# Sixteen short rows ahead: splitting the first load of a decode step's keys

## The chip, the core and the metric

The kernel runs on one core of one Trainium2 chip. The metric is the device time of one execution in microseconds, as the median of several runs. A profile of one execution stands beside it: what each engine did and when, and what moved through the DMA queues. The engines are PE (matrix products; PEld is its loading of weights), DVE, ACT, POOL, and SP, which here only issues transfers between HBM and the on-chip memory. That memory has 128 rows; a transfer writes a stretch of bytes into each of the rows that it names.

## The reference

One token for each of 4 sequences passes an attention block over a cache and an MLP, both with a residual. Everything is in float32.

```python
B, Sq, D = 4, 1, 448;  Hq, Hkv, Sk, Dh = 16, 8, 4096, 256
W = min(4096, max(256, Sk // 4))                       # 1024: the last keys and values only
q = (x @ wq).reshape(B, Sq, Hq, Dh).transpose(0, 2, 1, 3)
k = jnp.repeat(k_cache[:, :, Sk - W:, :], rep, axis=1)  # rep = 2 query heads for each of 8
v = jnp.repeat(v_cache[:, :, Sk - W:, :], rep, axis=1)
scores = jnp.einsum("bhqd,bhkd->bhqk", q, k) * (Dh ** -0.5)
o = jnp.einsum("bhqk,bhkd->bhqd", _softmax(scores), v)
...
h = x + A(_layernorm(x))            # A ends with: heads side by side, times wo
h2 = h + B(_layernorm(h))           # B: layernorm, gelu(y @ w1 + b1) @ w2 + b2
```

Keys and values of 8 heads and 1024 positions and the weights make 88.2 MB that are read once.

## The kernel before, in words

All data is packed on the host so that each load is a block of 128 rows. The 8 key and value heads are handled in four pairs. For a pair, PE forms the queries from `wq` (`project`, `queries`), multiplies them with the keys (`scores`), and DVE and ACT take the softmax (`softmax`, `transpose_p`). Then PE multiplies with the values (`values`) and with `wo` (`outputs`). After the last pair the MLP follows with `w1` and `w2`.

The loads go through three large slots of on-chip memory (`ring`, tiles `slot`). Each holds up to 65,024 bytes per row, and the loads take the slots in turn: `t0`, then `l1` to `l8`, then the last three (`te0` to `te2`) with the last keys and values, `wo`, `w1` and `w2`. All are issued by SP in program order. A load that reuses a slot waits on SP until PE has read what lay there. The first slot, `t0`, receives two loads: `wq0` (the query weights of head 0, and with them `x` and the two bias vectors, 7312 bytes per row), and behind it `k0` (the keys of head 0, 32768 bytes per row, and 6144 bytes with the first three quarters of the query weights of head 1). The rest of those weights comes in two small transfers of 32 rows x 2048 bytes into `wq1_last`. `l1` and `l2` follow into the other two slots and wait for nothing.

The order on each engine is the order of the code. A recorder (`Machine`) notes every operation with the parts of memory that it reads and writes, and `emit` gives each the semaphore waits that it needs. It follows a write by rows (in groups of four) and columns, and every transfer has a semaphore of its own (`landed_N`, N being the operation's number). So an operation that reads columns that two transfers wrote waits for both. All operations are emitted at line 75, which is why nearly all rows of the profile say L75; tiles tell them apart.

In the front of the program, `x` is normalised (`centred`, `column_mean`, `rsqrt`), the queries of heads 0 and 1 are formed, and the scores of head 0 begin:

```python
    t = slot("t0")
    wqt, xT, b2T, b1T = cut(load(t, 0, wq0), (WEIGHTS, ND * B, 4, 4 * 4))
    ...
    ka, kb, wqt1 = cut(load(t, WEIGHTS + COLUMNS, k0), (HALF, HALF, 3 * 512))
    ...
    project(pq, wq_parts(yT[1], wqt1, wq1_last), False)
    queries(0, pq)
    s = score_tiles(0)
    for h, kt in enumerate((ka, kb)):
        scores(s, 0, h, keys(kt))
```

Of the kernel before, what the change touches and what calls it, by code (L numbers as in the profile page):

```python
# [24 lines left out]
HALF = CACHE // 2  # L25
WEIGHTS = 4 * D
SLOT = CACHE + 2 * WEIGHTS + HALF
COLUMNS = ND * B + 4 + 4 * 4
# [169 lines left out]
        return flat.rearrange(f"p ({names}) -> p {names}", **{f"a{i}": n for i, n in enumerate(shape[1:])})  # L198


def block_kernel(nc, wq0, k0, wq1, l1, l2, l3, l4, l5, l6, l7, l8, k7, vo, v7, wo, w1, w2, out):
    real, nc = nc, Machine(nc)

    def rows_of_tag(name, shape, dtype):
# [16 lines left out]
    def slot(name):  # L221
        return ring.tile([P, SLOT], F32, tag="slot", name=name)

    def load(t, at, src, pieces=None):
        dst = t[:, at : at + src.shape[-1]]
        at = 0
        for n in pieces or (src.shape[-1],):
            nc.sync.dma_start(dst[:, at : at + n], src[:, at : at + n])
            at += n
        return dst  # L230

    def cut(t, sizes):
        parts, at = [], 0
        for n in sizes:
            parts.append(t[:, at : at + n])
            at += n
        return parts


    def wq_parts(y, t, last=None):  # L240
        parts = [(a, y[:, a, :], slice(0, 512), t[:, a * 512 : (a + 1) * 512]) for a in range(3)]
        if last is not None:
            return parts + [(3, y[:H, 3, :], slice(0, 512), last)]
        for i in range(2):
            parts.append((3, y[:, 3 + i, :], slice(i * 2 * P, (i + 1) * 2 * P), t[:, 3 * 512 :]))
        return parts
# [9 lines left out]
    def output_weights(t):  # L256
# [6 lines left out]
        out=ident, in_=ident, compare_op=ALU.not_equal, fill=1.0, base=0, pattern=[[-1, P]], channel_multiplier=1  # L263
# [187 lines left out]


    t = slot("t0")
    wqt, xT, b2T, b1T = cut(load(t, 0, wq0), (WEIGHTS, ND * B, 4, 4 * 4))
    wqt = wq_parts(yT[0], wqt)
    xT = xT.rearrange("p (a b) -> p a b", a=ND)
    ka, kb, wqt1 = cut(load(t, WEIGHTS + COLUMNS, k0), (HALF, HALF, 3 * 512))
    for i in range(2):
        nc.sync.dma_start(
            wq1_last[i * Q : (i + 1) * Q, :], wq1[i].rearrange("e (p c) -> e p c", c=512)[:, :4, :]  # L460
# [44 lines left out]
    ka, kb, va = cut(load(slot("l1"), 0, l1), (HALF, HALF, HALF))  # L505
# [8 lines left out]
    vb, v, wo_a, wo_b = cut(load(slot("l2"), 0, l2), (HALF, CACHE, WEIGHTS, WEIGHTS))  # L514
# [5 lines left out]
    wq_a, wq_b, ka, kb, k2 = cut(load(slot("l3"), 0, l3), (WEIGHTS, WEIGHTS, HALF, HALF, HALF))  # L520
# [7 lines left out]
    k2, v, wq_a, wq_b = cut(load(slot("l4"), 0, l4), (HALF, CACHE, WEIGHTS, WEIGHTS))  # L528
# [8 lines left out]
    v, wo_a, wo_b, ka = cut(load(slot("l5"), 0, l5), (CACHE, WEIGHTS, WEIGHTS, HALF))  # L537
# [6 lines left out]
    kb, ka, k2 = cut(load(slot("l6"), 0, l6), (HALF, HALF, HALF))  # L544
# [7 lines left out]
    v, va, wq_a, wq_b = cut(load(slot("l7"), 0, l7), (CACHE, HALF, WEIGHTS, WEIGHTS))  # L552
# [6 lines left out]
    vb, wo_a, wo_b, ka, kb = cut(load(slot("l8"), 0, l8), (HALF, WEIGHTS, WEIGHTS, HALF, HALF))  # L559
# [9 lines left out]
    v, wot = cut(load(e[1], 0, vo), (CACHE, 2 * D))  # L569
# [138 lines left out]
    for c in range(first, NFC - 1):  # L708
        g = gT[:, c, :] if c < 12 else gT_last[:, c - 12, :]
        for j in range(4):  # L710
            m, n = (Q, 2) if c == first else (B, 2 if j < 3 else 1)
# [5 lines left out]
    for part, of in ((0, slice(0, 3)), (1, slice(3, 4))):  # L717
        for j in range(4):
            n = P // 4 if j < 3 else H // 4
# [89 lines left out]
```

## Time and profile before

| what | value |
|---|---|
| time, median of 3 runs | 211.96 us (211.85 to 212.13) |
| time of the profiled execution | 211.87 us |
| its span, first to last instruction | 210.6 us |
| PE busy | 139.0 us (66%), 984 matmuls |
| DVE, ACT, POOL busy | 28.8, 14.4, 5.0 us |
| moved by DMA | 88.42 MB in 3400 packets, mean 420 GB/s |
| load of `wq0`, of `k0` | 914 KB in 4.8 us, 4864 KB in 15.9 us from issue to landing |

Times in views of the trace count from the start of the span. The two rows of digits for the DMA show the span in 40 equal slices: the busy share of the 16 DMA engines in tenths, and the GB/s that they moved. A packet is counted, with all its bytes, in the window or slice in which it starts, so short windows can show a share above 1. In rows of the timeline, what stands in brackets is how long the engine sat idle before, and what ended that.

### The profile page before, as it was taken

The numbers are of one execution on the slowest core, as the hardware profiler recorded it, in microseconds if no ns is written. First come the engines' busy times: TensorE is split into PE (matmuls) and PEld (weight loads), VectorE is DVE, ScalarE is ACT, GpSimd is POOL, SyncE is SP. The second block draws the span as 40 slices with busy tenths as digits, with TensorE's granted clock in tenths as the row PEclk, the third lists the DMA queues.
The fourth block names the chain that finished last, engine by engine and source line by source line (L and its number), as shares of the span: only waits on it lengthen the run. The fifth ranks groups of instructions, "written<-read, shape, count | busy, mean of one in ns | idle before, by whom it ended". The sixth has DMA issues, their size and how long they took to land.

```text
span 210.6 us, 2206 instructions
## 1 busy us (share of the span) xinstructions
PE 139.0 (66%) x984; PEld 47.2 (22%) x984; DVE 28.8 (14%) x135; ACT 14.4 (7%) x34; POOL 5.0 (2%) x17
## 2 busy tenths in 40 slices
PE   0467759621971679198359775419806999888996
PEld 0420202200220223034012222102301233224332
DVE  7210101300020011013001104000100213012320
ACT  2010000200000010020000002000100002010311
POOL 5100000000000000000000000000000000000100
PEclk9999996996799559969967999757965899999999
DMA  7999999899999999999999999999999999999993
GB/s 296 429 399 473 448 492 389 386 436 507 398 398 410 531 389 410 410 519 398 413 411 448 481 398 425 434 470 398 434 411 442 416 428 429 425 407 439 424 409 138
DMA packets 3400, 88.42 MB, mean 420 GB/s; under 512 B 512, under 2 KB 768, under 8 KB 1344
## 3 DMA queue, kind: packets, MB, share of 16 engines
q1 hardware_dynamic: 3392, 88.30, 97.6%
q8 instruction: 7, 0.11, 0.2%
q14 instruction: 1, 0.01, 0.0%
HBM read 88.23 MB, written 0.07 MB: 419 GB/s over the span
## 4 chain that ended last, share of the span: by engine, by line
DMA 77%; PE 18%; SPq 2%; DVE 1%; issue 1%; ACT 0%
DMA slot<-l 64%; DMA slot<-w 14%; PE b_o L75 9%; PE b_s L75 4%; PE b_acc L75 3%; SPq L75 2%; PE b_m L75 1%; DVE oT L75 1%; DVE w_o L75 0%; PE b_t L75 0%; DVE o_u L75 0%; ACT o_u L75 0%; DVE o_res L75 0%
## 5 line engine op out<-in xcount | busy, mean ns | idle before, releaser
L75 PE MATMUL b_o<-slot,pT 128*32 128x512 f32 x224 | 33.6, 752 | 29.3 <-DMA slot<-l 28.5
L75 PE MATMUL b_s<-slot,qT 128*32 128x512 f32 x256 | 36.6, 722 | 10.4 <-DMA slot<-l 9.1
L75 PE MATMUL b_m<-slot,yT 128*32 128x512 f32 (+1 forms) x76 | 11.9, 734 | 11.5 <-DMA slot<-l 6.4
L75 PEld LDWEIGHTS b_o<-slot,pT 128*32 128x32 f32 x224 | 7.8, 132 | 51.4 <-DMA slot<-l 30.9
L75 PE MATMUL b_t<-idle 128*32 128x512 bf16 x64 | 18.1, 404 | 0.5 <-DVE pT L75 0.5
L75 PEld LDWEIGHTS b_s<-slot,qT 128*32 128x32 f32 x256 | 8.8, 128 | 35.9 <-issue 22.5
L75 ACT ACTIVATE o_p<-b_s,w_nm 128x512 f32<-128x512 f32 x8 | 5.4, 682 | 93.1 <-DVE w_nm L75 93.1
L75 DVE TENSOR_REDUCE w_mx<-b_s 128x1 f32<-128x512 f32 x8 | 5.5, 692 | 43.7 <-PE b_s L75 43.7
L75 DVE TENSOR_SCALAR w_o<-b_o,w_rec 128x512 f32<-128x512 f32 x4 | 3.0, 751 | 52.5 <-PE b_o L75 52.5
L75 PEld LDWEIGHTS b_m<-slot,yT 128*32 128x32 f32 x76 | 4.3, 142 | 17.9 <-DMA slot<-l 6.9
L75 PEld LDWEIGHTS b_t<-idle 128*32 128x32 bf16 x64 | 5.9, 100 | 10.3 <-issue 5.8
L75 DVE TENSOR_REDUCE w_sm<-b_m 128x32 f32<-128x128 f32 x4 | 1.2, 291 | 48.2 <-PE b_m L75 48.2
L75 PE MATMUL b_t<-ident,o_p 128*128 128x128 f32 x32 | 5.0, 285 | 4.0 <-ACT o_p L75 3.9
L75 PE MATMUL b_acc<-slot,oT 128*32 128x448 f32 x52 | 6.1, 545 | 1.9 <-DVE oT L75 1.9
L75 ACT COPY w_qs<-b_m 128x512 f32<-128x512 f32 x4 | 2.3, 584 | 60.8 <-PE b_m L75 60.8
L75 POOL TENSOR_TENSOR o_r<-w_ve,mhalf 128x1 f32<-128x1 f32 x2 | 1.1, 542 | 189.0 <-DVE w_ve L75 189.0
L75 PE MATMUL b_m<-ident,w_qs 128*128 128x128 f32 x16 | 3.5, 361 | 2.9 <-ACT w_qs L75 2.9
L75 PEld LDWEIGHTS b_t<-ident,o_p 128*128 128x128 f32 x32 | 3.4, 141 | 7.4 <-ACT o_p L75 7.4
L75 PE MATMUL b_m<-slot,mean 128*128 128x12 f32 (+1 forms) x4 | 1.1, 370 | 5.6 <-DMA slot<-wq 5.6
L75 PE MATMUL b_o<-slot,yT 128*32 128x512 f32 x10 | 4.6, 594 | 0.0
L75 PE MATMUL b_m<-ident,w_o 128*128 128x128 f32 x20 | 3.3, 286 | 1.8 <-DVE w_o L75 1.8
L75 DVE COPY pT<-b_t 128x16 f32<-128x16 f32 x32 | 3.3, 167 | 6.0 <-PE b_t L75 6.0
(94 smaller groups left out, 66.7 us busy)
## 6 DMA issues: line engine op xcount, KB each, us to landing
slot<-l SPq DMA_DIRECT2D x6, 7936.0 KB, 43.0
slot<-l SPq DMA_DIRECT2D x2, 6144.0 KB, 34.1
slot<-k SPq DMA_DIRECT2D x1, 4864.0 KB, 15.9
slot<-vo SPq DMA_DIRECT2D x1, 4544.0 KB, 33.1
slot<-k SPq DMA_DIRECT2D x1, 4096.0 KB, 43.5
slot<-v SPq DMA_DIRECT2D x1, 3072.0 KB, 19.0
slot<-w SPq DMA_DIRECT2D x1, 2240.0 KB, 28.6
slot<-w SPq DMA_DIRECT2D x1, 1792.0 KB, 34.0
```

Of the source, the lines that this page charges most:

```text
L75: self.machine.add(Op(self.name, lambda: getattr(issuer, what)(*args, **kwargs), outs, ins, what))
```

## The change

The load `k0` is cut into three. Of the first 14336 bytes of each row (`kf`, the first 7 of 16 parts of the keys), 16 rows are loaded before `wq0`, and the other 112 rows behind it. The rest of the columns, 24576 bytes per row, follows as the new `k0`. They land in the same places as before, so what the engines read is unchanged.

```diff
     t = slot("t0")
+    n = kf.shape[-1]
+    k0t = t[:, WEIGHTS + COLUMNS :][:, : n + k0.shape[-1]]
+    nc.sync.dma_start(k0t[:16, :n], kf[:16])
     wqt, xT, b2T, b1T = cut(load(t, 0, wq0), (WEIGHTS, ND * B, 4, 4 * 4))
     wqt = wq_parts(yT[0], wqt)
     xT = xT.rearrange("p (a b) -> p a b", a=ND)
-    ka, kb, wqt1 = cut(load(t, WEIGHTS + COLUMNS, k0), (HALF, HALF, 3 * 512))
+    nc.sync.dma_start(k0t[16:, :n], kf[16:])
+    nc.sync.dma_start(k0t[:, n:], k0)
+    ka, kb, wqt1 = cut(k0t, (HALF, HALF, 3 * 512))
...
-        "wq0": np.concatenate([wq[0], xT, b2, b1], axis=1), "k0": k0, "wq1": wq1, ...
+        "wq0": np.concatenate([wq[0], xT, b2, b1], axis=1), "kf": k0[:, : 7 * 512], "k0": k0[:, 7 * 512 :], "wq1": wq1, ...
```

On SP, at the start of the program, the transfers stand so (rows x elements of 4 bytes; a minus is before, a plus is after):

```order
-L75 DMA slot<-wq 128x1828 [waits barrier_Pool_Activation_PE_DVE_SP_release]
-L75 DMA slot<-k 128x9728
+L75 DMA slot<-kf 16x3584 [waits barrier_Pool_Activation_PE_DVE_SP_release]
+L75 DMA slot<-wq 128x1828
+L75 DMA slot<-kf 112x3584
+L75 DMA slot<-k 128x6144
 L75 DMA wq_last<-wq 32x1x512 x2
 L75 DMA slot<-l 128x12288
```

The 16 rows take the place behind the start barrier, `wq0` is second, and all that follows is two issues later.

On PE, from the second head's query weights to the first scores (`b_m` holds the queries, `b_s` the scores; 26 is the landing of the 16 rows, 28 that of the 112, and `k0` has the number 27 before and 29 after):

```order
-L75 MATMUL b_m<-slot,yT 32x512 [waits landed_27]
+L75 MATMUL b_m<-slot,yT 32x512 [waits landed_29]
 L75 MATMUL b_m<-slot,yT 32x512 x2
-L75 MATMUL b_m<-wq_last,yT 32x512 [waits landed_28,landed_29]
+L75 MATMUL b_m<-wq_last,yT 32x512 [waits landed_30,landed_31]
 L75 MATMUL b_m<-ident,w_qs 128x128 [waits done_ACT]
 L75 MATMUL b_m<-ident,w_qs 128x128 x3
-L75 MATMUL b_s<-slot,qT 32x512 [waits done_DVE]
+L75 MATMUL b_s<-slot,qT 32x512 [waits landed_28,landed_26,done_DVE]
 L75 MATMUL b_s<-slot,qT 32x512 x15
```

The projection waits for the last of the pieces as it did for the whole, and the first score matmul has two waits more, for the two pieces of `kf`. No other instruction on PE, DVE, ACT or POOL has moved.

More of the change, by code (lines that the diff above doesn't have):

```diff
@@ L198, in tile, with block_kernel @@
         return flat.rearrange(f"p ({names}) -> p {names}", **{f"a{i}": n for i, n in enumerate(shape[1:])})
-def block_kernel(nc, wq0, k0, wq1, l1, l2, l3, l4, l5, l6, l7, l8, k7, vo, v7, wo, w1, w2, out):
+def block_kernel(nc, wq0, kf, k0, wq1, l1, l2, l3, l4, l5, l6, l7, l8, k7, vo, v7, wo, w1, w2, out):
     real, nc = nc, Machine(nc)
@@ L795 @@
     arrays = {
-        "wq0": np.concatenate([wq[0], xT, b2, b1], axis=1), "k0": k0, "wq1": wq1, **loads, "k7": k[7], "vo": vo, "v7": v[7], "wo": wo_end, "w1": w1, "w2": w2,
+        "wq0": np.concatenate([wq[0], xT, b2, b1], axis=1), "kf": k0[:, : 7 * 512], "k0": k0[:, 7 * 512 :], "wq1": wq1, **loads, "k7": k[7], "vo": vo, "v7": v[7], "wo": wo_end, "w1": w1, "w2": w2,
     }
```

## The prediction

> **What bounds the kernel now.** I read the page first: the slices, the DMA queues, the chain that ended last.
>
> ```profile
> DMA  7999999899999999999999999999999999999993
> GB/s 296 429 399 473 448 492 389 386 436 507 398 398 410 531 389 410 410 519 398 413 411 448 481 398 425 434 470 398 434 411 442 416 428 429 425 407 439 424 409 138
> q1 hardware_dynamic: 3392, 88.30, 97.6%
> DMA 77%; PE 18%; SPq 2%; DVE 1%; issue 1%; ACT 0%
> DMA slot<-l 64%; DMA slot<-w 14%; PE b_o L75 9%; PE b_s L75 4%; PE b_acc L75 3%; SPq L75 2%; PE b_m L75 1%; DVE oT L75 1%; DVE w_o L75 0%; PE b_t L75 0%; DVE o_u L75 0%; ACT o_u L75 0%; DVE o_res L75 0%
> ```
>
> The DMA engines are busy in 38 of 40 slices; one queue carries 88.3 MB and fills 97.6% of the span of 16 engines. The chain runs 77% of the span through loads. So the kernel is one stream of bytes, and PE works beside it. The stretches of the stream, from the view of busy time by window (last two columns: DMA share, GB/s):
>
> ```profile
> core 0: us, PE busy (x) PEld busy (x) DVE busy (x) ACT busy (x) POOL busy (x), PEclk, DMA share, GB/s
> 1.50:1.70 0.20, 0.00 (x0) 0.00 (x0) 0.17 (x2) 0.20 (x1) 0.20 (x2) 1.00 0.00 0
> 1.70:2.10 0.40, 0.00 (x0) 0.00 (x0) 0.37 (x3) 0.31 (x1) 0.40 (x4) 1.00 1.24 219
> 2.10:2.50 0.40, 0.00 (x0) 0.00 (x0) 0.40 (x3) 0.00 (x0) 0.40 (x2) 1.00 0.59 128
> 2.50:2.90 0.40, 0.00 (x0) 0.00 (x0) 0.40 (x1) 0.00 (x0) 0.40 (x2) 1.00 0.71 256
> 2.90:3.30 0.40, 0.00 (x0) 0.00 (x0) 0.40 (x1) 0.00 (x0) 0.40 (x2) 1.00 1.09 457
> 17.00:200.00 183.00, 125.03 (x847) 40.03 (x847) 21.52 (x103) 10.64 (x26) 0.89 (x2) 0.86 1.00 430
> 206.80:208.00 1.20, 1.20 (x48) 0.84 (x40) 0.00 (x0) 0.53 (x1) 0.00 (x0) 1.00 0.39 138
> ```
>
> From 17 to 200 us the stream has a share of 1.00 at 430 GB/s, which is 26.9 GB/s for each of 16 engines. It begins at 1.7 us, and it still moves bytes after 206.8. What waits for its end:
>
> ```profile
> 206.64 0.56 PEld L75 LDWEIGHTS b_o<-slot,gT 128*32 128x32 f32 x24 [0.63 <-DMA slot<-w]
> 207.85 0.73 PE L75 MATMUL b_o<-slot,gT_last 128*4 128x64 f32 x24
> 208.66 0.29 DVE L75 TENSOR_TENSOR o_res<-b_o,o_hb 128x128 f32<-128x128 f32 x1 [4.31 <-PE b_o L75]
> 208.97 0.35 SPq L75 DMA_DIRECT2D out<-o_res  x1
> ```
>
> The last matmuls use the last pieces of `w2`, some 0.7 us behind the last bytes, then come one addition and the store. Nothing lies between that could take up a delay: a stream that ends a microsecond later ends the kernel about a microsecond later. The profiled execution took 211.87 us with a span of 210.6, 0.09 under the median of 211.96; the sum is made against 211.87.
>
> **The change, part by part.** No byte is added. The order in the queue is changed, and one load of 4864 KB becomes three, of 16 rows x 14336 bytes, 112 rows x 14336 and 128 rows x 24576. Issues and waits in the front of the program:
>
> ```profile
> 0.73 0.39 SPq L75 DMA_DIRECT2D slot<-wq  x1
> 1.18 0.41 SPq L75 DMA_DIRECT2D slot<-k  x1
> 1.64 1.55 SPq L75 DMA_DIRECT2D wq_last<-wq  x2
> 3.23 39.24 SPq L75 DMA_DIRECT2D slot<-l  x4
> 17.13 1.93 PE L75 MATMUL b_m<-slot,yT 128*32 128x512 f32 x6 [3.33 <-DMA slot<-k]
> PE b_m L75 <- DMA slot<-wq: 5.6, 1, 5.6
> PE b_m L75 <- DMA slot<-k: 3.3, 1, 3.3
> PE b_s L75 <- DMA slot<-l: 2.3, 1, 2.3
> ```
>
> *Two more issues on SP.* An issue to all 128 rows takes 0.39 to 0.41 us, with 0.05 to the next, so `wq0` is issued 0.45 us later (1.18) and the pair for `wq1_last` and `l1` some 0.9 later (`l1` at 4.1). `l1` is needed in the queue when `wq0` and the keys are through: 5.92 MB at 430 GB/s are 13.8 us behind 1.7, so about 15.5. Eleven microseconds of queued work hide the later issues; `l2` follows directly, and all further loads wait for PE and not for SP's turn. Zero.
>
> *`wq0` lands later.* It holds `x` and the first weights, and PE waits 5.6 us for it. Behind the 16 rows it lands 0.5 to 2.2 us later. The normalisation and the first projection come after it, but then PE waits 3.3 us for the keys' load, whose tail holds the second weights: that wait is the cover, and up to 3.3 us cost nothing. Even beyond it, PE waits 2.3 us for `l1` after the first scores, and the slot of the first keys, which the third load needs, is next written when `l1` and `l2` are through (14.4 MB, 34 us at 430 GB/s). Zero.
>
> *A wait added on PE.* The first score matmul now waits for the landings of the 16 and of the 112 rows as well. Behind it stand all scores of PE. Both are ahead of the last piece in the queue, and the projections before the scores already wait for that piece. Zero, unless the last piece lands before them; the cover is then the 2.3 us above.
>
> *More packets.* Each engine moves 8 rows of a load to 128 rows. It gets 8 packets more (two short rows for a long one) and two landings more. The shortest packets of the stream, the 2 KB rows of `wq1_last`, show what a packet costs:
>
> ```profile
> DMA packets 19, 0.03 MB, mean 205 GB/s; under 512 B 3, under 2 KB 3, under 8 KB 19
> q1 hardware_dynamic: 19, 0.03, 53.6%
> ```
>
> These are the queue's rows for 16.20 to 16.36 us, where only 16 such packets and 3 landings start: 53.6% of 16 engines for 0.16 us is 1.37 us of packet time, 86 ns for each 2 KB at most, where 2048 bytes at 26.9 GB/s need 76. Some 10 ns for a packet, times 10: **+0.10 us**.
>
> *The start of the stream.* Between 1.7 and 3.3 us it moved 219, 128, 256 and 457 GB/s in steps of 0.4 us. Against 430 it lacks (211 + 302 + 174 - 27) x 0.4 = 264 KB, which is 0.61 us. This is all that an earlier or better filled start could win. With 16 rows, each engine can have one packet of 14336 bytes (0.53 us at 26.9 GB/s), about as long as the 0.45 us until the next issue. The gain has bounds of 0 and 0.61. I take all of it, **-0.61 us**, since whatever is slow in these 1.6 us now runs under a transfer that in my forecast takes longer than that anyway.
>
> *The 16 rows themselves.* No transfer of the trace goes to 16 rows. One end: all 16 engines carry a row each at 26.9 GB/s, 0.53 us. Other end: a row receives no more than in a transfer to 128 rows, 430/128 = 3.4 GB/s, which makes 54 GB/s for 16 rows and 229 KB in 4.27 us, 3.73 more. The nearest row is the one above: the transfer to 32 adjacent rows filled 8.6 of 16 engines and moved 205 GB/s, so 32 rows took the bytes of about eight engines, one for four rows, and nothing in the trace shows several engines writing into the same few rows at full rate. Sixteen rows at half of 205 are 102 GB/s: 2.24 us, **+1.70 us** over the 0.53. It is on the path, since every engine stands on its one row until then and the stream behind it moves back. [...]
>
> *The 112 rows.* At 430 GB/s 1.61 MB take 3.73 us; at the 128-row pace per row (376 GB/s) 4.27. Bounds 0 and, if they crowd as the 16 do, several microseconds. Nearest is the load to 128 rows, so I take the second value, **+0.53 us**.
>
> *The 128 rows of 24576 bytes* go at the stream's rate: zero beyond the packets counted.
>
> Sum: +0.10 - 0.61 + 1.70 + 0.53 = +1.72; 211.87 + 1.72 = **213.6 us**.
>
> **The rivals.** *The start is won (faster, the other side).* If 16 engines write their 16 rows side by side at 26.9 GB/s, nothing crowds, and each engine has work from 1.7 us on while `wq0` is issued: up to -0.61 + 0.10 = -0.51, 211.4 us. For it speak the weak 128 to 256 GB/s in the start, which look like engines without work, and that the row is as long as an issue. Against it, that the trace has no such transfer and the 0.61 must be won nearly whole. It decides when the 16 rows land in under about 0.7 us of stream.
>
> *The start is paid once (no change).* The slow 1.6 us may belong to the first bytes of any transfer into an empty queue. Then the 16 rows take the place of `wq0` in it, without crowding: +0.10 and at most 0.5 won, 211.6 to 212.0, 211.9 in the middle of what I hold likely. For it, the queue's rows of the first 1.2 us:
>
> ```profile
> DMA packets 33, 0.24 MB, mean 201 GB/s; under 512 B 0, under 2 KB 0, under 8 KB 33
> q1 hardware_dynamic: 33, 0.24, 84.7%
> ```
>
> In 1.7 to 2.9 us 33 packets account for 84.7% of the engines' time at half the rate: work is there and is slow. Against it: this does not tell waiting for a request from waiting for bytes.
>
> *The 112 rows crowd too.* Seven adjacent rows for an engine don't line up with groups of four; at half pace their 3.73 us double: 213.6 - 0.5 + 3.7 = 216.8 us.
>
> **How the numbers follow.** A change under 0.2% (0.42 us) can't be told from none here. The forecast, crowding by 16 rows, has 0.50: nothing shows the contrary, and it needs one mechanism. The won start 0.25, the start paid once 0.18, the heavier crowding 0.07. So slower 0.57, the same 0.18, faster 0.25. The forecast's own range: crowding half as strong, without the 112 rows (+0.85 - 0.4 + 0.1 = 0.5), 212.4, up to 2.24 us without any win at the start and with a share of 1.5 us on the 112 rows (+1.7 + 0.1 + 1.5), 215.2. For 8 in 10 the range goes down to the won start, 211.3, and stops at 215.2, which leaves out the heavy crowding and little else.
>
> **What would show it.** Right: in the first slice fewer GB/s, about 100 in the 2 us after the first bytes; the wait for `wq0` 7 us or more instead of 5.6; the keys landing at 18 to 19 us instead of 17.1; the chain of waits as before; the whole tail moved by the same amount. The start won: over 300 GB/s from 1.7 us on, keys before 16.9. Wrong in another way: a gap in the DMA row where a load waits for a slot, or a tail no longer bound by `w2`.

## The result, and the profile after

The changed kernel takes 215.0 us (median of four runs, 214.94 to 215.43), the kernel before, run beside it, 211.93: a ratio of 1.0148, with a 95% interval of 1.013 to 1.0166, so 3.1 us slower. The profiled execution took 214.94 us with a span of 213.6, which is 3.0 over the span before.

First the page of the changed kernel: DMA share and rate in 40 slices, the queue, and the chain that ended last.

```profile
DMA  6999999899999999999989999999998999999993
GB/s 170 335 382 466 442 442 454 383 464 465 392 428 487 404 407 452 464 404 404 490 375 423 433 458 455 440 416 464 392 440 387 463 429 418 413 410 438 432 406 129
q1 hardware_dynamic: 3552, 88.30, 97.6%
DMA 78%; PE 17%; SPq 2%; DVE 1%; issue 1%; ACT 0%
```

The bytes and the chain are as before, and the queue has 160 packets more: 128 rows and 32 landings. The share of the engines' time is the same 97.6%, of a longer span. The rate fell only in the front, from 296, 429, 399 to 170, 335, 382 GB/s in the first three slices; a share of 9 with a low rate means that packets were under way and moved slowly. The same in windows of the changed kernel (last two columns: DMA share, GB/s):

```profile
1.70:2.10 0.40, 0.00 (x0) 0.00 (x0) 0.37 (x3) 0.31 (x1) 0.40 (x4) 1.00 2.28 502
2.10:2.50 0.40, 0.00 (x0) 0.00 (x0) 0.40 (x3) 0.00 (x0) 0.40 (x2) 1.00 0.28 72
2.50:2.90 0.40, 0.00 (x0) 0.00 (x0) 0.40 (x1) 0.00 (x0) 0.40 (x2) 1.00 1.04 110
2.90:3.30 0.40, 0.00 (x0) 0.00 (x0) 0.40 (x1) 0.00 (x0) 0.40 (x2) 1.00 1.09 146
6.30:11.30 5.00, 2.24 (x8) 2.00 (x8) 0.87 (x5) 0.00 (x0) 0.97 (x1) 1.00 0.96 275
17.00:200.00 183.00, 120.32 (x824) 38.52 (x824) 20.55 (x98) 9.06 (x23) 0.00 (x0) 0.83 1.00 432
```

Between 1.7 and 2.5 us all 16 short rows start (that they are counted whole in the window of their start makes the 502), and then little follows: 110 and 146 GB/s where the kernel before had 256 and 457. The second slow place is 6.3 to 11.3 us, 275 GB/s at a full share; the queue's rows for that window show what moves there:

```profile
DMA packets 96, 1.38 MB, mean 275 GB/s; under 512 B 0, under 2 KB 0, under 8 KB 0
q1 hardware_dynamic: 96, 1.38, 96.0%
```

96 packets in 1.38 MB are 14336 bytes each: as many as six rows of the 112 for each of 16 engines. At 96.0% of 16 engines for 5 us one takes 800 ns, where 26.9 GB/s would make it 533. From 17 us on the stream runs at 432 GB/s, as before. What SP, PE and the end show, with the lines in the order of time:

```profile
4.17 41.63 SPq L75 DMA_DIRECT2D slot<-l  x4
6.91 1.12 PE L75 MATMUL b_m<-slot,mean 128*128 128x12 f32 x4 [6.91 <-DMA slot<-wq]
19.89 1.93 PE L75 MATMUL b_m<-slot,yT 128*32 128x512 f32 x6 [4.81 <-DMA slot<-k]
35.02 5.34 PE L75 MATMUL b_s<-slot,qT 128*32 128x512 f32 x32 [3.92 <-DMA slot<-l]
209.71 0.56 PEld L75 LDWEIGHTS b_o<-slot,gT 128*32 128x32 f32 x24 [0.63 <-DMA slot<-w]
211.72 0.29 DVE L75 TENSOR_TENSOR o_res<-b_o,o_hb 128x128 f32<-128x128 f32 x1 [4.33 <-PE b_o L75]
```

PE gets the first weights 1.28 us later (6.91 for 5.63), the last of the keys' load 2.76 later (19.89 for 17.13), and at the end the same instructions come 3.07 and 3.06 us later (209.71 for 206.64, 211.72 for 208.66). Nearly all is lost before 20 us, and it is carried through the stream to the end undiminished.

### The profile page after: what moved, and what is told of

Read it like the earlier page. It is cut to its first block, busy times and chain, and to the rows that moved or that the text cites. A ratio compares the mean times of both kernels' runs of the same rounds, so it can differ in the third digit from the quotient of the medians.

```text
span 213.6 us, 2209 instructions
## 1 busy us (share of the span) xinstructions
PE 137.2 (64%) x984; PEld 47.0 (22%) x984; DVE 28.8 (13%) x135; ACT 14.5 (7%) x34; POOL 5.0 (2%) x17
## 3 DMA queue, kind: packets, MB, share of 16 engines
q1 hardware_dynamic: 3552, 88.30, 97.6%
## 4 chain that ended last, share of the span: by engine, by line
DMA 78%; PE 17%; SPq 2%; DVE 1%; issue 1%; ACT 0%
DMA slot<-l 64%; DMA slot<-w 14%; PE b_o L75 9%; PE b_acc L75 3%; PE b_s L75 3%; SPq L75 2%; PE b_m L75 1%; DVE oT L75 1%; DVE w_o L75 0%; PE b_t L75 0%; DVE o_u L75 0%; ACT o_u L75 0%; DVE o_res L75 0%
## 5 line engine op out<-in xcount | busy, mean ns | idle before, releaser
L75 PE MATMUL b_s<-slot,qT 128*32 128x512 f32 x256 | 35.3, 699 | 15.3 <-DMA slot<-l 13.8
```

The source lines that it names most:

```text
L75: self.machine.add(Op(self.name, lambda: getattr(issuer, what)(*args, **kwargs), outs, ins, what))
```

## The experiments

All are changes to the kernel before. "More" is an additional load that nothing reads, into the unused end of the first slot; its rows are 14144 bytes, 192 under the 14336 of the change, since the free end of the slot doesn't hold the longer row (a slot has 63,488 bytes per row, not the 65,024 given above). It is issued behind the keys where nothing else is said, so it moves in the midst of the stream. Each comparison is with runs of the kernel before on the same chip. The cuts of code show the transfers alone; the definitions of `n`, `k0t` and `spare` and the packing on the host are left out.

**Cut, but to all rows.** Is it the number of pieces?

```diff
-    ka, kb, wqt1 = cut(load(t, WEIGHTS + COLUMNS, k0), (HALF, HALF, 3 * 512))
+    nc.sync.dma_start(k0t[:, :n], kf)      # 128 rows x 14336 bytes, behind wq0
+    nc.sync.dma_start(k0t[:, n:], k0)
+    ka, kb, wqt1 = cut(k0t, (HALF, HALF, 3 * 512))
```

> The keys' first 14336 bytes per row are a load of their own to all 128 rows, behind the first query weights; nothing is ahead of them. Crowding theory (transfers to 16 and to 112 adjacent rows make several DMA engines write into the same few rows): no crowding here, only 8 packets and one landing more per engine, +0.1 us, 212.0. Split theory (the loss comes from cutting one load into short pieces): most of the loss of the change stays, 213.5 or more. Start theory (the loss comes from short transfers into the empty queue): 212.0 as in the first.

Measured: 212.13 against 211.91 us, ratio 1.0008 (0.9999 to 1.0018). Cutting costs about 0.2 us, and by the interval no more than 0.4. The split theory falls.

**The same pieces behind the weights.** Is it the place at the start?

```diff
     wqt, xT, b2T, b1T = cut(load(t, 0, wq0), (WEIGHTS, ND * B, 4, 4 * 4))
-    ka, kb, wqt1 = cut(load(t, WEIGHTS + COLUMNS, k0), (HALF, HALF, 3 * 512))
+    nc.sync.dma_start(k0t[:16, :n], kf[:16])
+    nc.sync.dma_start(k0t[16:, :n], kf[16:])
+    nc.sync.dma_start(k0t[:, n:], k0)
+    ka, kb, wqt1 = cut(k0t, (HALF, HALF, 3 * 512))
```

> The same three pieces as in the change (16 rows, 112 rows, the rest), but all behind the first query weights and x, so the queue starts as before the change. Crowding theory: the pieces cost the same or more, as nothing of the slow start runs under them: +2.5 to +3.5 us, 214.4 to 215.4. Start theory: the loss is gone, 212.0 to 212.3. Split theory: about as e1_split_128 plus one landing.

Measured: 216.82 against 211.91, +4.9 us, ratio 1.0234 (1.0219 to 1.0249). The start theory falls: away from the start the same pieces cost more, by 1.8 us, than in the change. The window in which they move, of this run:

```profile
5.20:13.20 8.00, 4.01 (x18) 2.60 (x18) 1.96 (x11) 0.00 (x0) 1.03 (x1) 1.00 1.02 223
```

Eight microseconds at a share of 1.02 and 223 GB/s, half of the stream's rate with the engines marked as busy. The time also came out above the range that I gave for crowding (214.4 to 215.4).

**The same bytes in the midst of the stream, in one transfer and in two.**

```diff
     ka, kb, wqt1 = cut(load(t, WEIGHTS + COLUMNS, k0), (HALF, HALF, 3 * 512))
+    nc.sync.dma_start(spare, more)             # one transfer
...
+    nc.sync.dma_start(spare[:16], more[:16])   # or two
+    nc.sync.dma_start(spare[16:], more[16:])
```

> As before the change, with one load more that nothing reads: 128 rows x 14144 bytes (1.81 MB) into the unused end of the first slot, behind the keys. It is the yardstick for e5_more_16_112. All theories: 1.81 MB at 430 GB/s, +4.2 us, 216.1.

> The same additional bytes into the same place at the same point of the queue, in two transfers, of rows 0 to 15 and of rows 16 to 127, in the midst of a full stream. Crowding theory: 2.5 to 3.5 us over e4_more_128 (1.6 for the 16 rows, 1 to 2 for the 112), 218.6 to 219.6. Start theory: e4_more_128 plus 0.05, since the queue is full. Split theory: e4_more_128 plus 0.1.

Measured: 216.26 us in one transfer (ratio 1.0207, 1.019 to 1.0224), 221.04 in two (1.0431, 1.0416 to 1.0447), against 211.91. The yardstick, +4.35 us, is what the bytes take; the two transfers cost 4.8 more, again over the range given (its 1.6 us for the 16 rows was an estimate; alone they lose 2.2, as the next runs show). So the loss comes in the midst of the stream as well, with the same bytes in the same place; what differs is which rows each transfer names, and that there is one transfer more. The next runs separate these.

**The 16 rows alone, to adjacent rows and spread.** Is it the target rows, or that 16 rows are few, or that adjacent source rows are read at once?

```diff
+    nc.sync.dma_start(spare[:16], more)         # rows 0 to 15
...
+    nc.sync.dma_start(spare[0:106:7], more)     # or every seventh row
...
+    nc.sync.dma_start(spare[0:61:4], more)      # or every fourth row
```

> As before the change, with one additional transfer of 16 rows x 14144 bytes (226 KB) to the adjacent rows 0 to 15 of the unused end of the first slot, in the midst of the stream; nothing reads it. The bytes alone are 0.53 us. Crowding theory: 16 engines write into rows that four engines serve in a load to 128 rows, 2.2 us, so 213.7 to 214.2. If only the 112 rows crowd: 212.5.

> The same 16 source rows, one per engine, but written to every seventh row (0, 7, ... 105). Crowding by target rows: the rows lie apart, nearly nothing is left, 212.5 (0.53 us for the bytes). Rival, the transfer is slow because it has 16 rows or because 16 adjacent source rows are read at once: the same as e6_more_16.

> The same 16 source rows written to every fourth row (0, 4, ... 60): 16 different groups of four, all in the lower half of the rows. If only a group of four rows is shared, nothing crowds: 212.5, as e7_more_16_spread. [...]

Measured, against 212.01: 214.73 for adjacent rows (ratio 1.0129, 1.0114 to 1.0144), 213.02 for every seventh (1.0048, 1.0031 to 1.0065), 213.12 for every fourth (1.0051, 1.0036 to 1.0066). So +2.72, +1.01 and +1.11 us for the same source rows and the same 0.53 us of bytes. The first scores with `l1` show the stream behind the transfer; the kernel before first, then adjacent rows, then every seventh:

```profile
31.71 5.31 PE L75 MATMUL b_s<-slot,qT 128*32 128x512 f32 x32 [2.28 <-DMA slot<-l]
34.98 5.92 PE L75 MATMUL b_s<-slot,qT 128*32 128x512 f32 x32 [4.28 <-DMA slot<-l]
32.84 5.13 PE L75 MATMUL b_s<-slot,qT 128*32 128x512 f32 x32 [2.93 <-DMA slot<-l]
```

The loss lies with the target rows: spread apart, 1.7 of the 2.2 us that adjacent rows cost beyond their bytes are gone. Source rows, row count and the number of transfers are the same in both, so none of them explains it. A fixed pace for each row is out as well: at the 3.4 GB/s of the prediction's other end a row of 14144 bytes takes 4.2 us, and the spread rows cost 1.01. Adjacent and spread rows alike came out some 0.5 us above what was expected. Every seventh against every fourth row makes no difference that these runs can tell (213.02 and 213.12): both lost 0.5 to 0.6 us beyond their bytes.

**The 112 rows alone.**

```diff
+    nc.sync.dma_start(spare[16:], more[16:])
```

> The additional transfer goes to rows 16 to 127 alone (112 rows x 14144 bytes, 1.58 MB; 3.7 us at 430 GB/s, 215.6). Crowding theory with seven adjacent rows for each engine, out of step with the groups in which a load to 128 rows is dealt out: 2 to 3.5 us more, 217.6 to 219.1; with the forecast's 0.5 it is 216.1. If the 16 rows ahead of it had caused its slow packets in e5_more_16_112: 215.7.

Measured: 218.18 against 212.01, +6.17 us, ratio 1.029 (1.0275 to 1.0305). The bytes are 3.7, so 2.5 are lost. With 2.2 for the 16 rows that makes 4.7, and both together had cost 4.8. The 112 rows alone take longer than all 128 rows in the same place did (6.17 us against 4.35). The queue's window behind the first rows of that transfer, of this run:

```profile
16.90:20.90 4.00, 1.93 (x6) 0.20 (x6) 0.00 (x0) 0.00 (x0) 0.00 (x0) 1.00 1.02 272
```

272 GB/s, nearly the 275 that the 112 rows had in the change.

**Half of the rows.** Do they get the whole rate, with four rows for each engine?

```diff
+    nc.sync.dma_start(spare[:64], more)
```

> As before the change, with one additional transfer of 64 rows x 14144 bytes (905 KB) to rows 0 to 63 in the midst of the stream: four adjacent rows for each engine, so every engine has a group of four rows to itself. Its bytes are 2.1 us at 430 GB/s. If only several engines in one group of four rows are slow: 214.1 to 214.4. [...] If any transfer to fewer than 128 rows pays in proportion to its packets (e10_more_112 paid 2.5 us for seven packets per engine): 2.1 + 1.4, 215.5.

Measured: 216.98 against 211.99, +4.99 us, ratio 1.0236 (1.0219 to 1.0253). From 17 to 19 us only rows of this transfer start, 32 of the 64:

```profile
q1 hardware_dynamic: 32, 0.45, 111.8%
```

111.8% of 16 engines for 2 us is 1118 ns for a row, where 26.9 GB/s would make it 526: 16 engines at this pace move 202 GB/s, half of the stream's 430. The row of this run for 16.9 to 20.9 us:

```profile
16.90:20.90 4.00, 1.93 (x6) 0.20 (x6) 0.00 (x0) 0.00 (x0) 0.00 (x0) 1.00 1.04 225
```

That is 225 GB/s at a share of 1.04, so 216 for 16 engines that are busy throughout, again half. The whole transfer cost 2.9 us beyond its 2.1 us of bytes, somewhat more than a doubling of that time. The 214.1 to 214.4 us of a limit that lies only in groups of four adjacent rows are out, as far as each engine had four adjacent ones. No trace says which engine writes which row: that, the groups in which rows are dealt out and the four engines for rows 0 to 15 were assumptions of mine that no run shows. A price by the number of packets alone, 215.5, is out too.

**At the start: 16 adjacent rows, 16 spread rows, and short pieces of all rows.**

```diff
+    nc.sync.dma_start(spare[:16], more)         # ahead of wq0; keys whole
...
+    nc.sync.dma_start(spare[0:106:7], more)     # or spread, ahead of wq0
...
+    nc.sync.dma_start(k0t[:, :n], kf)           # or 1792 bytes of all 128 rows of keys
     wqt, xT, b2T, b1T = cut(load(t, 0, wq0), (WEIGHTS, ND * B, 4, 4 * 4))
```

> The additional transfer of 16 adjacent rows (226 KB, read by nothing) stands ahead of the first query weights; the keys are loaded whole as before the change. In the midst of the stream it cost 2.7 us. If the slow start runs under it (the forecast's 0.61 us taken in full): 214.1. If all that the place ahead saved between e3_pieces_behind and the change (1.8 us) belongs to the 16 rows: 212.9 to 213.0. If nothing is saved: 214.7.

> The same 16 rows ahead, written to every seventh row. In the midst of the stream it cost 1.0 us. Start won: 0.4 us or less is left over before, 212.4 or less (its bytes alone are 0.53). Start paid once by whatever comes first: 212.5 to 213.0. The rows decide as in the midst: e8_more_16_ahead is 1 us or more above it; if not, the start hides the crowding.

> 229 KB of the keys are ahead of the first query weights as in the change, but as 1792 bytes of all 128 rows; the rest of the keys follows as one load. Crowding theory: no loss from the pieces, only 8 packets and a landing more per engine (e1_split_128 measured +0.2 us for that), and what an early transfer wins at the start: 211.6 to 212.1. If being ahead of the weights costs by itself (the weights land later): 212.5 or more.

Measured, against 212.03: 213.51 for adjacent rows (ratio 1.0066, 1.0052 to 1.008), 212.95 for spread ones (1.0038, 1.0025 to 1.0051), 212.07 for the short pieces of all rows (1.0002, 0.9993 to 1.0011). At the start the adjacent rows cost 1.48 us with 0.53 of bytes, so 0.95, where in the midst of the stream they cost 2.2: the place at the start is some 1.2 us cheaper. That the slow start covers a part of the crowding fits, since adjacent rows lose only 0.56 us against spread ones here, and 1.71 in the midst. But all of it can't be so, as the start lacks no more than 0.61 us of bytes; the rest is open. Nothing is seen to be won by going ahead. The short pieces of all rows leave the time as it was (by the interval, 0.15 us faster to 0.23 slower), and the start of that run looks so:

```profile
1.70:2.10 0.40, 0.00 (x0) 0.00 (x0) 0.37 (x3) 0.31 (x1) 0.40 (x4) 1.00 0.89 108
2.10:2.50 0.40, 0.00 (x0) 0.00 (x0) 0.40 (x3) 0.00 (x0) 0.40 (x2) 1.00 0.56 202
2.50:2.90 0.40, 0.00 (x0) 0.00 (x0) 0.40 (x1) 0.00 (x0) 0.40 (x2) 1.00 1.29 420
```

The first 0.8 us are as slow as in the kernel before (108 and 202 GB/s here, 219 and 128 there). This other form of the first transfer doesn't fill them. No version came out faster than the kernel before.

## Why the prediction was right, and where its sizes were off

The direction holds, and so does crowding of adjacent rows as a cause: 213.6 us was forecast with 211.3 to 215.2 as the range, and 215.0 came out, just inside it. The time moved by 3.1 us where the sum had 1.72, and the larger part of it arose where the forecast had put little: the 112 rows cost about 2.1 us for a term of 0.53. That they crowd was a rival, with a chance of 0.07.

*The 16 rows with the start* (forecast -0.61 and +1.70, together +1.09): 0.95 measured at the start. That the two agree is in good part luck, for the row from which the +1.70 was worked out doesn't show what was read in it. It was said that 32 rows take the bytes of only about eight engines, as 205 GB/s were moved and 8.6 engines filled. But the window counts only packets that start in its 0.16 us. The row of the kernel before for the 7 us around it is the stream at its full rate:

```profile
13.00:20.00 7.00, 3.67 (x12) 0.77 (x10) 0.00 (x0) 0.88 (x2) 0.00 (x0) 1.00 1.00 430
```

And each packet to the 32 rows took 86 ns by the prediction's own working, which is 24 GB/s for an engine, near its whole 26.9. Moreover the landings suggest that only eight engines took part in each of the two small transfers. A transfer to 128 rows has 16 landing packets (the two additional pieces of the change have brought 128 rows and 32 landings), and the page's 3392 packets are 23 transfers of 128 rows with 16 landings each, 64 short rows, and 16 landings, 8 for each small transfer. If each engine that takes part has one landing, eight engines moved the bytes at nearly their own pace; either way no limit of the rows is seen.

In place of that step the runs show this. Adjacent rows cost 1.71 us more than spread ones in the midst of the stream, which is the size of the term by coincidence, and a further 0.5 that spread rows cost too is missing in the sum. At the start the whole is 1.2 us less. The gain of 0.61 was not one that an early transfer could win, as the short pieces of all rows show; the cheaper place at the start stands where the sum had it. Nor did every engine stand on its one row for 2.24 us. These are the queue's rows of the changed kernel for 1.7 to 2.5 us, with the 16 short rows, and for 2.5 to 3.3, with 14 rows of the first weights and 14 landings:

```profile
q1 hardware_dynamic: 16, 0.23, 128.1%
q1 hardware_dynamic: 28, 0.10, 106.7%
```

The short rows took 1.02 us each in the mean, and the rows behind them nearly as long (0.98 us with the landings counted in), though they have 7312 bytes; between 2.9 and 3.3 us of the kernel before such a row took 0.28 us. So a part of the delay is seen in what is queued behind.

*The 112 rows* (forecast +0.53): this is the mis-sized term. They cost 2.5 us in the midst of the stream alone, and in the change about 2.1, which is what 3.1 leaves after the 0.95, with the price of cutting in it. I had priced them by the 128-row pace per row, a pace that the spread rows have shown not to be a limit. Why they crowd is not shown: no run wrote 112 rows in another arrangement. The rival for this had the kind of the loss right and went too far in size: its 3.7 us would have made 216.8. Its groups of four rows were read from the same window as the +1.70, and no run shows them.

*More packets* (+0.10): the cut alone cost 0.2 us, with an interval that holds both zero and 0.10.

*The costs set to zero* held: with the normalisation and the first projection done, PE still waited 4.81 us for the keys' load, and later 3.92 for `l1`, so neither the later weights nor the additional waits were on the path. SP issued `l1` at 4.17, as forecast (4.1).

*The start won* and *the start paid once*, the two rivals with no crowding, are out for the change, which loses. The second of them described the start better: the short pieces of all rows, put first, won nothing that could be measured.

*The signs listed ahead* came in the direction told, with sizes off: the wait for the first weights was 6.91 us (7 or more was said), the keys came at 19.89 instead of 18 to 19, the tail moved as a whole, and the rate after the first bytes was lower, though 177 GB/s rather than 100 over the two microseconds, which is this row of the changed kernel:

```profile
1.70:3.70 2.00, 0.00 (x0) 0.00 (x0) 1.95 (x6) 0.31 (x1) 1.79 (x7) 1.00 1.02 177
```

Left open: the pieces behind the weights cost 4.9 us and in the change 3.1, and the 16 rows explain 1.2 of these 1.8. Why the 112 rows, too, are some 0.4 to 0.6 cheaper in the change was not tried, and of the 1.2 at most half is the slow start. Nor was it settled why spread rows still cost about 0.5 us.

## What to carry to other kernels

In a kernel that is one stream of loads, write every load to all 128 rows, as far as these runs go, and cut it along the columns if it must be cut. Here 112 rows took not 7/8 of the time of 128 but more than the whole (6.17 us against 4.35), and 64 rows ran at half rate. A busy DMA row with a low rate in the midst of the stream is the sign of it; at the start of the stream the row looked so without any narrow transfer (84.7% at 201 GB/s before the change). An additional transfer that nothing reads, put into the midst of the stream, prices a shape in one run beside its yardstick. And a rate in a short window says nothing of a limit until it is known how many engines took part.

## What the runs showed of the hardware that I had not expected

A narrow transfer cost more than I had reckoned. The 16 adjacent rows lost 2.2 us in the midst of the stream, of which 1.71 go away when the rows are spread; the 64 rows lost 2.9, where doubling their 2.1 us of bytes would lose 2.1. And the slow first microsecond of the stream, 0.61 us worth of bytes, is not a lack of issued work: with short pieces of all rows issued first and the weights right behind (the first two issues stand at 0.74 and 1.19 us in the changed kernel, both ahead of the first bytes at 1.7), the first 0.8 us moved 108 and 202 GB/s all the same.
